# A tile of its own for the normalised tokens of a half, and attention pairs inserted one FFN step sooner

## The chip, the cores and the metric

The kernel runs on one core of one Trainium2 chip. The metric is device microseconds (us) of one execution. TensorE (PE) does the matrix products, VectorE (DVE) and ScalarE (ACT) the elementwise work, GpSimd (POOL) small helpers, and SyncE (SP) issues every transfer (DMA).

## The reference, cut to what matters

```python
# attention: 8 batches, 8 heads, 512 local + 32 global tokens, head dim 64
s_ll = np.where(abs(pos_q - pos_k) <= 32, scale * q_l @ k_l.T, -1e9)
a_l = softmax(concat([scale * q_l @ k_g.T, s_ll]))      # local queries: global keys + a band
out_l = a_l @ concat([v_g, v_l])
out_g = softmax(scale * q_g @ concat([k_g, k_l]).T) @ concat([v_g, v_l])
x = concat([out_g, out_l])                               # (8, 544, 512)
# feed-forward part (FFN), 512 -> 2048 -> 512
xn = (x - mean(x)) / sqrt(var(x) + 1e-6) * g_ln
out = x + relu(xn @ w_ch1) @ w_ch2
```

## The kernel before, in words

A **half** is 256 local tokens of one batch. Two halves make a **chunk** of 512 tokens. There are nine chunks: 0 to 7 of local tokens, and chunk 8 with the 256 global tokens. `ffn(c, ...)` runs the FFN of chunk c over 16 **FFN steps** f (`for f in range(NF)`), one for each block of 128 of the 2048 hidden columns. Values and weights are split into a high and a low part, so each product is three matmuls. Step f has two parts on PE: `mm1(f)`, 12 matmuls of 512 columns (L673), into one of two PSUM banks `ph`, after which ACT writes `hh` (relu, L681) and DVE `hl` (the rest, L682); and `mm2(f - 1, t)` for the four token tiles t, 12 matmuls (L692) that read hh and hl of the step before. Step 0 has no mm2, and after step 15 comes `mm2(15, t)` by itself, with the residual added by DVE (L723) and the rows stored.

The attention for chunk c + 1 is done during the FFN of chunk c. Its unit is a `Pair`, two pairs of heads of one half, four units to a chunk. Code that a unit needs is a generator, and `step()` advances the generator at the head of the queue `side` by one piece: three times in each mm1 and once ahead of each mm2(.., t), so seven times in an FFN step. `attend(u, before, spread)` is such a generator: it issues the scores of pair u (PE L378, 64 small matmuls), the value products of the pair before it (PE L443), their normalisation into `x` (DVE L461), the mask and minimum of the scores (DVE L397) with the exponentials (ACT L407), and then, in chunks 1 to 6, 32 transposes of 32-row blocks on DVE (L430), two to a piece. `at`, filled by `put(place, run)`, says where a generator starts: place 2f + k is step f, ahead of mm1 (k = 0) or ahead of its mm2 (k = 1). In chunks 1 to 6 it is `put(2 * f + 1, ...)` for f in `PAIR_STEPS`; in chunk 0, where the weights are still being split by DVE and ACT, it is a spacing of its own, and the transposes are a second generator (`u.transposes`).

When the pair that ends a half has its values, its `values()` stores the 256 rows to a DRAM scratch `xs` (L335, read back as residual by L701 at step 14 of the chunk's own FFN) and then runs `norm`: statistics (DVE L188, L190), the reciprocal root (POOL L192, L193), a small product (DVE L198), and two ACT activations that write the normalised tokens (L203). `attend` places these with

```python
ends = before.at[1] == HP - 2 if before else False
...
if ends and n in (0, 5, 7):
    next(sums, None)                 # n=0: store, statistics; 5: L198 and L203; 7: second L203
elif next(turns, turns) is turns:    # two block transposes on DVE
    break
```

The tiles `x` come from `new_x()`, a ring of buffers. At step 15 `next_chunk()` transposes the normalised tokens of chunk c + 1 on PE (L621, four times four matmuls, one group ahead of each mm2(14, t)); each group takes one of two PSUM banks `t` (tag `att`, shared with the scores), which ACT (`xh`, L633) and DVE (`xl`, L634) empty.

The order of SP's queue and, from chunk 0 on, of PE is the program's order. For DVE, ACT and POOL it is the program's order in chunks 1 to 6; ahead of these and behind them a scheduler orders their instructions. Chunk 7 has the attention of the global tokens (`Global`) inserted, from its first FFN step on.

Of the kernel before, what the change touches and what calls it, by code (L numbers as in the profile page):

```python
# [17 lines left out]
AF = mybir.ActivationFunctionType  # L18
# [12 lines left out]
SPLIT_AHEAD = 3  # L31
LOADS_AHEAD = 2

PAIR_STEPS = (1, 5, 9, 13)
BIG = 3.0e38


# [8 lines left out]
def attention_ffn_kernel(  # L46
# [130 lines left out]

        return load, split

    def norm(x, js, xn=None):  # L180

        n = len(js)
        at = slice(js[0], js[-1] + 1)
        mv = small.tile([P, 2, 2], F32, name="mv")
        rs = small.tile([P, 2, 2], F32, name="rs")
        st = small.tile([P, 2, 1, 6], F32, name="st")
        for j in js:
            nc.vector.bn_stats(st[:, j, 0, :], x[:, j, :])  # L188
        for j in js:
            nc.vector.bn_aggr(mv[:, j, :], st[:, j])  # L190
        y = rs[:, 0, at]
        nc.gpsimd.tensor_scalar(y, mv[:, at, 1], EPS, None, ALU.add)  # L192
        nc.gpsimd.tensor_tensor(y, y, neg_half[:, :n], op=ALU.pow)  # L193

        def apply():
            yield
            if xn is None:
                nc.vector.scalar_tensor_tensor(  # L198
                    rs[:, 1, at], mv[:, at, 0], -1.0, rs[:, 0, at], ALU.mult, ALU.mult
                )  # L200
            for j in js:
                if xn is None:
                    nc.scalar.activation(  # L203
                        x[:, j, :], x[:, j, :], AF.Identity,
                        bias=rs[:, 1, j:j + 1], scale=rs[:, 0, j:j + 1],
                    )
                else:
                    nc.vector.tensor_scalar(
                        xn[:, j, :], x[:, j, :], mv[:, j, 0:1], rs[:, 0, j:j + 1],
                        ALU.subtract, ALU.mult,  # L210
                    )
                yield

        return apply()

    xtags = cycle(["x0", "x1", "x2"])

    def new_x():
        return fpool.tile([P, 2, DM], F32, name="x", tag=next(xtags))

    class Local:
# [76 lines left out]
        def values(self):  # L298
            b, hp, half = self.at

            pv = self.bank(3, "pv")
            for h in range(2):
                for qb in range(2):
                    for g in range(4):
                        gp = slice(g * WIN, (g + 1) * WIN)
                        nc.tensor.matmul(
                            pv[gp, qb * P + h * D:qb * P + h * D + D],
                            self.pt[:, 2 * h + qb, gp],
                            self.v[:, 4 * qb + g, h * D:(h + 1) * D],
                            start=True,  # L310
                            stop=True,
                            tile_position=(0, g * WIN),
                            skip_group_check=True,
                        )
            ri = small.tile([P, 4], F32, name="ri")
            nc.gpsimd.tensor_scalar(ri, self.sm, SUM_EPS, None, ALU.add)
            nc.vector.reciprocal(ri, ri)
            nc.vector.tensor_tensor(
                self.x[:, :, hp * P:(hp + 1) * P].rearrange("p q (h d) -> p q h d", h=2),
                pv[:, :256].rearrange("p (q h d) -> p q h d", q=2, h=2),  # L320
                ri.rearrange("p (h q) -> p q h", h=2).unsqueeze(3).to_broadcast([P, 2, 2, D]),
                op=ALU.mult,
            )
# [13 lines left out]
    class Pair:  # L337
# [96 lines left out]
        def values(self):  # L434
            b, hp, half = self.at
            pv = ps_h.tile([P, 512], F32, name="pv", tag="ph")
            for j in range(2):
                for h in range(2):
                    for qb in range(2):
                        for g in range(4):  # L440
                            gp = slice(g * WIN, (g + 1) * WIN)
                            at = (2 * j + qb) * P + h * D
                            nc.tensor.matmul(  # L443
                                pv[gp, at:at + D],
                                self.pt[:, j, 2 * h + qb, gp],
                                self.v[:, j, 4 * qb + g, h * D:(h + 1) * D],
                                start=True,
                                stop=True,
                                tile_position=(0, g * WIN),
                                skip_group_check=True,  # L450
                            )
            ri = small.tile([P, 2, 4], F32, name="ri2")
            nc.gpsimd.tensor_scalar(ri, self.sm, SUM_EPS, None, ALU.add)
            if self.next_pair:
                self.next_pair.load_values()
            else:
                begin(1)
            yield
            nc.vector.reciprocal(ri, ri)
            for j in range(2):  # L460
                nc.vector.tensor_tensor(  # L461
                    self.x[:, :, (hp + j) * P:(hp + j + 1) * P].rearrange(
                        "p q (h d) -> p q h d", h=2
                    ),
                    pv[:, j * 256:(j + 1) * 256].rearrange("p (q h d) -> p q h d", q=2, h=2),
                    ri[:, j].rearrange("p (h q) -> p q h", h=2)
                    .unsqueeze(3).to_broadcast([P, 2, 2, D]),
                    op=ALU.mult,
                )
            yield  # L470
            if hp == HP - 2:
                store_x(b, half, self.x)
                yield from norm(self.x, range(2))

    def load_global_keys(ap, bg, hp):
        kr = ap.tile([P, BG, SA], F32, name="gk")
# [285 lines left out]
    ready = {}  # L762
# [41 lines left out]
    def attend(u, before, spread):  # L804

        sums = values(before) if before else iter(())
        scores = u.scores() if u else iter(())
        next(scores, None)
        next(sums, None)
        next(scores, None)  # L810
        next(sums, None)
        yield
        for _ in scores:
            yield
        turns = u.transposes() if u and spread else iter(())
        ends = before.at[1] == HP - 2 if before else False
        n = 0
        while True:
            if ends and n in (0, 5, 7):
                next(sums, None)  # L820
            elif next(turns, turns) is turns:
                break
            n += 1
            yield
        for _ in sums:
            pass
# [60 lines left out]
    for c, chunk in enumerate(chunks):  # L887
        if c == 0:
            ctx.enter_context(tc.manual_schedule(engines={ET.PE}))
        if c == 1:  # L890
            ctx.enter_context(tc.manual_schedule(engines={ET.SP}))
            rest = ExitStack()
            rest.enter_context(tc.manual_schedule(engines={ET.DVE, ET.Activation, ET.Pool}))
        if c == last_chunk - 1:
            rest.close()
        if chunk is None:
            rows = [rows_global(bg) for bg in range(NBG)]
        else:
            rows = [rows_local(b, 2 * half + j) for b, half in chunk for j in range(2)]
        at = {}  # L900

        def put(place, run):
            at.setdefault(min(int(place), 2 * NF - 1), []).append(run)

        if c == 0:
            for n in range(len(PAIR_STEPS) + 1):
                u, before = new.pop(0)
                put(1 + 6.5 * n, lambda u=u, before=before: attend(u, before, False))
                put(3 + 6.5 * n, u.transposes)
        elif c < last_chunk - 1:  # L910
            for f in PAIR_STEPS:
                u, before = new.pop(0)
                put(2 * f + 1, lambda u=u, before=before: attend(u, before, True))
        elif c < last_chunk:
            for n, u in enumerate(phases[1]):
                for o, run in enumerate(global_stages(u)):
                    put(1 + 3.5 * n + o, run)

        def stage(f, k, at=at, c=c):
            if c == 0 and k == 0:  # L920
                for _ in weights_to(f + SPLIT_AHEAD + 1, LOADS_AHEAD):
                    pass
            for run in at.get(2 * f + k, ()):
                yield from run()

        nxt = []

        def next_chunk(c=c, nxt=nxt):
            if c + 1 < len(chunks):
                yield from transpose_chunk(tiles(c + 1), nxt)  # L930

        ffn(c, xt, rows, stage, next_chunk)
        xt = nxt
# [89 lines left out]
```

## Time and profile before

| what | us |
|---|---|
| median of three runs | 987.63 (985.41 to 989.88) |
| the profiled execution | 988.89 |
| its span, first to last instruction | 987.1 |
| PE busy in the span | 933.2 |
| DVE busy | 571.0 |
| ACT busy | 312.9 |

The profiled execution lasts 1.8 us longer than its span, and is 1.3 us above the median. Engines run side by side, each in its own order; an engine that stands still costs time only where the one that sets the end waits for it. The granted clock is TensorE's, as a share of full speed (1.00 is 2.4 GHz, 0.50 is 1.2 GHz), as a mean over a stretch.

### The profile page before, as it was taken

The numbers are of one execution on the slowest core, as the hardware profiler recorded it, in microseconds if no ns is written. First come the engines' busy times: TensorE is split into PE (matmuls) and PEld (weight loads), VectorE is DVE, ScalarE is ACT, GpSimd is POOL, SyncE is SP. The second block draws the span as 40 slices with busy tenths as digits, with TensorE's granted clock in tenths as the row PEclk, the third lists the DMA queues.
The fourth block names the chain that finished last, engine by engine and source line by source line (L and its number), as shares of the span: only waits on it lengthen the run. The fifth ranks groups of instructions, "written<-read, shape, count | busy, mean of one in ns | idle before, by whom it ended". The sixth has DMA issues, their size and how long they took to land.

```text
span 987.1 us, 20917 instructions
## 1 busy us (share of the span) xinstructions
PE 933.2 (95%) x8616; PEld 732.2 (74%) x8616; DVE 571.0 (58%) x1845; ACT 312.9 (32%) x842; POOL 38.4 (4%) x122
## 2 busy tenths in 40 slices
PE   6579998999999998999899999999899989999997
PEld 3348776887878886888688878778787866766796
DVE  4688966647585666666685758474866442222311
ACT  5677843222232322222322232222222121232210
POOL 3100100000000000000000000000000000000000
PEclk9769998999999998999999999999999999999999
DMA  8565542322332222222432243214322324544200
GB/s 355 203 256 195 220 156 93 115 93 71 136 114 91 73 82 97 72 93 72 136 114 93 72 136 115 93 72 136 112 69 80 134 105 147 191 142 140 92 27 21
DMA packets 39039, 118.78 MB, mean 120 GB/s; under 512 B 4256, under 2 KB 6304, under 8 KB 34848
## 3 DMA queue, kind: packets, MB, share of 16 engines
q1 hardware_dynamic: 38944, 117.46, 33.9%
q8 instruction: 67, 1.10, 0.4%
q14 instruction: 28, 0.23, 0.1%
HBM read 99.62 MB, written 17.83 MB: 119 GB/s over the span
## 4 chain that ended last, share of the span: by engine, by line
PE 76%; DVE 9%; DMA 9%; ACT 4%; issue 2%; SPq 0%; POOL 0%; ACTq 0%; DVEq 0%
PE acc L692 33%; PE ph L673 33%; DMA xs<-x 5%; DVE pt L430 3%; DMA raw<-in_wd 3%; PE pv L443 2%; PE sc L378 2%; PE pv L547 1%; DVE hl L682 1%; PE t L621 1%; ACT hh L681 1%; PE sc L499 1%; DVE p L397 1%; DMA u<-in_eu 1%; PE t L535 1%
## 5 line engine op out<-in xcount | busy, mean ns | idle before, releaser
L692 PE MATMUL acc<-w,hh 128*128 128x512 f32 x1088 | 347.2, 401 | 0.0
L673 PE MATMUL ph<-xh,w 128*128 128x512 f32 (+1 forms) x1216 | 309.9, 382 | 3.6 <-ACT xh L633 2.6
L682 DVE SCALAR_TENSOR_TENSOR hl<-ph,hh 128x512 fp32r<-128x512 f32 (+1 forms) x144 | 95.3, 662 | 296.5 <-ACT hh L681 295.6
L673 PEld LDWEIGHTS ph<-xh,w 128*128 128x128 f32 x1216 | 217.7, 189 | 54.1 <-ACT xh L633 4.1
L692 PEld LDWEIGHTS acc<-w,hh 128*128 128x128 f32 x1088 | 209.2, 192 | 46.3
L430 DVE STREAM_TRANSPOSE pt<-p 32x128 f32<-32x128 f32 x768 | 232.1, 302 | 11.3
L692 PE MATMUL acc<-w,hl 128*128 128x512 f32 x544 | 226.6, 417 | 0.3 <-DVE hl L682 0.3
L681 ACT ACTIVATE hh<-ph 128x512 fp32r<-128x512 f32 (+1 forms) x144 | 82.2, 570 | 447.0 <-PE ph L673 447.0
L673 PE MATMUL ph<-xl,w 128*128 128x512 f32 x512 | 141.8, 398 | 0.0
L692 PEld LDWEIGHTS acc<-w,hl 128*128 128x128 f32 x544 | 104.7, 192 | 27.0 <-issue 2.6
L673 PEld LDWEIGHTS ph<-xl,w 128*128 128x128 f32 x512 | 96.6, 190 | 25.2 <-issue 1.8
L407 ACT ACTIVATE p<-p,mn 128x128 f32<-128x128 f32 x224 | 87.2, 391 | 27.5 <-DVE mn L397 27.5
L203 ACT ACTIVATE x<-x,rs 128x512 f32<-128x512 f32 x32 | 25.5, 810 | 90.1 <-DMA xs<-x 76.2
L397 DVE CUSTOM_DVE_ANT_0 p<-sc,mask 128x128 f32<-128x128 f32 x224 | 50.8, 284 | 0.0
L621 PE MATMUL t<-ident,x 128*128 128x128 f32 x136 | 26.6, 318 | 22.6 <-DVE xl L634 11.7
L621 PEld LDWEIGHTS t<-ident,x 128*128 128x128 f32 x136 | 19.3, 161 | 31.8 <-DVE xl L634 14.3
L407 ACT ACTIVATION_READ_ACCUMULATOR p<-p,mn 128x1 f32 x224 | 42.0, 187 | 0.0
L633 ACT ACTIVATE xh<-t,g_sb 128x512 fp32r<-128x512 f32 (+1 forms) x40 | 24.6, 621 | 31.0 <-PE t L621 30.8
L634 DVE SCALAR_TENSOR_TENSOR xl<-t,g_sb,xh 128x512 fp32r<-128x512 f32 (+1 forms) x36 | 24.1, 687 | 16.0 <-ACT xh L633 15.9
L378 PEld LDWEIGHTS sc<-e 64*32 64x32 f32 x1792 | 25.5, 107 | 10.5 <-issue 10.5
L378 PE MATMUL sc<-e 64*32 64x128 f32 x1792 | 33.2, 279 | 0.0
L443 PE MATMUL pv<-v,pt 128*32 128x64 f32 x1792 | 30.8, 220 | 0.0
(72 smaller groups left out, 497.7 us busy)
## 6 DMA issues: line engine op xcount, KB each, us to landing
v<-in_eu SPq DMA_DIRECT2D x28, 1024.0 KB, 7.2
e<-in_eu SPq DMA_DIRECT2D x28, 672.0 KB, 4.5
raw<-in_wd SPq DMA_DIRECT2D x16, 1024.0 KB, 5.4
gk<-in_gk SPq DMA_DIRECT2D x8, 1088.0 KB, 5.0
xs<-x SPq DMA_DIRECT2D x32, 256.0 KB, 7.0
ob<-xs SPq DMA_DIRECT2D x32, 256.0 KB, 6.9
out<-ob SPq DMA_DIRECT2D x32, 256.0 KB, 2.0
gv<-in_gv SPq DMA_DIRECT2D x8, 1024.0 KB, 4.9
```

Of the source, the lines that this page charges most:

```text
L203: nc.scalar.activation(x[:, j, :], x[:, j, :], AF.Identity, bias=rs[:, 1, j:j + 1], scale=rs[:, 0, j:j + 1],)
L378: nc.tensor.matmul(sc[h][gp, at:at + P], self.e[hd, j, w * WIN:(w + 1) * WIN], self.e[hd, j, k0 * WIN:(k0 + 4) * WIN], start=True, stop=Tr ...
L397: nc.vector.tensor_tensor_reduce(out=self.p[:, j, c], in0=sc[h][:, at:at + P], in1=masks[half, qb], scale=-QSCALE, scalar=BIG, op0=ALU.add ...
L407: nc.scalar.activation(self.p[:, j, c], self.p[:, j, c], AF.Exp, bias=mn[:, j, c:c + 1], scale=-1.0, accum_out=self.sm[:, j, c:c + 1],)
L430: nc.vector.transpose(out=self.pt[rp, j, :, gp], in_=self.p[gp, j, :, rp])
L443: nc.tensor.matmul(pv[gp, at:at + D], self.pt[:, j, 2 * h + qb, gp], self.v[:, j, 4 * qb + g, h * D:(h + 1) * D], start=True, stop=True, t ...
L621: nc.tensor.transpose(t[:, j * P:(j + 1) * P], xn[j][:, kt * P:(kt + 1) * P], ident)
L633: nc.scalar.activation(hi, t[:, :n], AF.Copy, scale=gk)
L673: nc.tensor.matmul(ph[:, :n], w[:, kt, :], xx[kt][:, :n], start=(i == 0), stop=(i == 3 * KT - 1),)
L681: nc.scalar.activation(hh[:, :n], ph[:, :n], AF.Relu)
L682: nc.vector.scalar_tensor_tensor(hl[:, :n], ph[:, :n], 0.0, f32(hh[:, :n]), ALU.max, ALU.subtract)
L692: nc.tensor.matmul(acc[t], a[:, ts], w, start=(f == 0 and i == 0), stop=(f == NF - 1 and i == 2),)
```

## The change

A pair that ends a half now writes its normalised tokens to a tile of its own (`xn`, which takes the place of `x` in `ready`), where before the activation wrote over `x`. The ring of tiles has four where it had three; a chunk takes four tiles in place of two. The activation is the same ACT instruction with another output. Second, the attends of chunks 1 to 6 start at FFN steps 0, 4, 8 and 12 in place of 1, 5, 9 and 13, and in chunk 0 at places 1, 7, 13, 19, 25 in place of 1, 7, 14, 20, 27 (their transposes at 3, 9, 15, 21, 27 in place of 3, 9, 16, 22, 29). Local units of chunk 0 and the global tokens keep their norm.

```diff
-PAIR_STEPS = (1, 5, 9, 13)
+PAIR_STEPS = (0, 4, 8, 12)
...
-    def norm(x, js, xn=None):
+    def norm(x, js, xn=None, act=False):
...
-            if xn is None:
+            if xn is None or act:
                 nc.vector.scalar_tensor_tensor(
                     rs[:, 1, at], mv[:, at, 0], -1.0, rs[:, 0, at], ALU.mult, ALU.mult
                 )
             for j in js:
-                if xn is None:
+                if xn is None or act:
                     nc.scalar.activation(
-                        x[:, j, :], x[:, j, :], AF.Identity,
+                        (xn if act else x)[:, j, :], x[:, j, :], AF.Identity,
                         bias=rs[:, 1, j:j + 1], scale=rs[:, 0, j:j + 1],
                     )
...
-    xtags = cycle(["x0", "x1", "x2"])
+    xtags = cycle(["x0", "x1", "x2", "x3"])
...
             if hp == HP - 2:
                 store_x(b, half, self.x)
-                yield from norm(self.x, range(2))
+                xn = ready[self.chunk][-1] = new_x()
+                yield from norm(self.x, range(2), xn, True)
...
-                put(1 + 6.5 * n, lambda u=u, before=before: attend(u, before, False))
-                put(3 + 6.5 * n, u.transposes)
+                put(1 + 6 * n, lambda u=u, before=before: attend(u, before, False))
+                put(3 + 6 * n, u.transposes)
```

## Rows read from the trace of the kernel before

**Rows 1.** The page, part 1: busy time of the engine, share of the span, instructions.
```profile
PE 933.2 (95%) x8616; PEld 732.2 (74%) x8616; DVE 571.0 (58%) x1845; ACT 312.9 (32%) x842; POOL 38.4 (4%) x122
```
**Rows 2.** Windows, chunks 0 to 6, cut where each chunk's mm1(0) starts.
```profile
core 0: us, PE busy (x) PEld busy (x) DVE busy (x) ACT busy (x) POOL busy (x), PEclk, DMA share, GB/s
...
72.70:179.17 106.47, 101.89 (x911) 80.94 (x910) 81.03 (x181) 60.49 (x124) 5.43 (x8) 0.95 0.44 159
179.17:281.42 102.25, 100.87 (x914) 80.64 (x913) 64.54 (x229) 28.23 (x88) 2.83 (x8) 1.00 0.29 98
281.42:388.35 106.93, 103.78 (x913) 82.84 (x913) 69.09 (x241) 28.16 (x88) 2.83 (x8) 0.97 0.28 98
388.35:494.68 106.33, 102.69 (x914) 81.88 (x913) 68.31 (x238) 28.16 (x88) 2.82 (x8) 0.98 0.29 96
494.68:596.92 102.24, 100.86 (x913) 80.70 (x913) 67.64 (x237) 28.24 (x88) 2.82 (x8) 1.00 0.28 98
596.92:702.36 105.44, 102.59 (x913) 81.85 (x913) 69.17 (x241) 28.23 (x88) 2.82 (x8) 0.98 0.29 99
702.36:802.53 100.17, 99.90 (x849) 79.72 (x849) 60.19 (x199) 24.96 (x72) 2.58 (x7) 1.00 0.29 100
```
**Rows 3.** Waits of the whole span: us in total, times, longest.
```profile
ACT x L203 <- DMA xs<-x: 76.2, 13, 7.3
...
PE t L621 <- DVE xl L634: 11.7, 5, 3.1
```
**Rows 4.** Timeline, end of chunk 2: start, us, engine, line, idle before.
```profile
364.39 1.19 SPq L335 DMA_DIRECT2D xs<-x  x2
...
369.05 0.16 DVE L198 SCALAR_TENSOR_TENSOR rs<-mv,rs 128x2 f32<-128x2 f32 x1
...
373.09 0.82 ACT L203 ACTIVATE x<-x,rs 128x512 f32<-128x512 f32 x1 [6.83 <-DMA xs<-x]
...
374.42 0.69 DVE L682 SCALAR_TENSOR_TENSOR hl<-ph,hh 128x512 fp32r<-128x512 f32 x1 [5.21 <-ACT hh L681]
...
375.14 3.79 DVE L430 STREAM_TRANSPOSE pt<-p 32x128 f32<-32x128 f32 x12
...
378.96 0.69 DVE L682 SCALAR_TENSOR_TENSOR hl<-ph,hh 128x512 fp32r<-128x512 f32 x1
379.57 1.40 DVE L634 SCALAR_TENSOR_TENSOR xl<-t,g_sb,xh 128x512 fp32r<-128x512 f32 x2
...
380.37 1.12 PE L621 MATMUL t<-ident,x 128*128 128x128 f32 x4 [3.06 <-DVE xl L634]
```
**Rows 5.** Windows, right behind that stall of chunk 2.
```profile
381.00:385.00 4.00, 4.00 (x14) 3.31 (x13) 1.38 (x2) 1.37 (x2) 0.00 (x0) 0.50 0.01 4
```
**Rows 6.** Timeline, last pair and end of chunk 1.
```profile
257.86 1.09 PE L673 MATMUL ph<-xh,w 128*128 128x512 f32 x4
...
259.61 0.69 DVE L682 SCALAR_TENSOR_TENSOR hl<-ph,hh 128x512 fp32r<-128x512 f32 x1 [4.91 <-ACT hh L681]
259.96 1.10 PE L443 MATMUL pv<-v,pt 128*32 128x64 f32 x64
...
266.80 0.16 DVE L198 SCALAR_TENSOR_TENSOR rs<-mv,rs 128x2 f32<-128x2 f32 x1
...
268.83 0.82 ACT L203 ACTIVATE x<-x,rs 128x512 f32<-128x512 f32 x1 [4.83 <-DMA xs<-x]
...
271.37 1.10 PE L673 MATMUL ph<-xh,w 128*128 128x512 f32 x4
...
276.11 0.66 PE L621 MATMUL t<-ident,x 128*128 128x128 f32 x4 [1.38 <-DVE xl L634]
```
**Rows 7.** Timeline, end of chunk 0, DVE and PE.
```profile
166.45 0.69 DVE L682 SCALAR_TENSOR_TENSOR hl<-ph,hh 128x512 fp32r<-128x512 f32 x1
...
167.83 0.16 DVE L198 SCALAR_TENSOR_TENSOR rs<-mv,rs 128x2 f32<-128x2 f32 x1
...
165.06 0.38 PE L621 MATMUL t<-ident,x 128*128 128x128 f32 x2
168.90 0.47 PE L621 MATMUL t<-ident,x 128*128 128x128 f32 x1 [3.45 <-ACT x L203]
...
179.01 1.10 PE L673 MATMUL ph<-xh,w 128*128 128x512 f32 x4
```
**Rows 8.** Timeline, end of chunk 6, from its first transposes to chunk 7's mm1(0).
```profile
794.93 0.60 PE L621 MATMUL t<-ident,x 128*128 128x128 f32 x4
...
802.37 1.10 PE L673 MATMUL ph<-xh,w 128*128 128x512 f32 x4
```
**Rows 9.** Windows, start of chunk 7, with a global unit inserted at step 0.
```profile
803.00:809.00 6.00, 4.00 (x42) 2.02 (x41) 2.44 (x9) 0.82 (x2) 0.00 (x0) 1.00 0.36 126
809.00:815.00 6.00, 5.33 (x22) 4.35 (x22) 0.75 (x5) 2.51 (x6) 0.23 (x1) 0.72 0.50 186
```

## The prediction

> **What bounds the kernel.** I read the page first: PE is busy 95% of the span [rows 1], so time can be won only where PE stands still or runs at half clock. Next the windows by chunk [rows 2]. Chunks 1 to 5 do the same work, yet last 102.2 to 106.9 us, and the long ones are those with a granted clock below 1.00. Chunk 6 lasts 100.2 and loses almost nothing. So several microseconds hang on something that happens in some chunks and not in others. The waits name it [rows 3]: PE's large wait is that of the transposes L621 for `xl` (11.7 us in five waits), one at the end of each of chunks 1 to 5, and on ACT the activation L203 waits 76.2 us for the store of `xs`.
>
> The timeline of chunk 2's end links the two [rows 4]. The store of x is issued at 364.39. The scale for L203 is ready at 369.05 + 0.16 = 369.21, but L203 writes over x and so starts only at 373.09, when the store has read it. ACT takes its instructions in order, so the `hh` of step 14 behind it is late, `hl` starts at 374.42, and twelve block transposes queued on DVE behind it end at 378.93. Only then come the `hl` of step 15 (378.96) and the first `xl` (379.57). The third group of PE transposes needs the bank that this `xl` empties: PE stands for 3.06 us, until 380.37. Thereafter the clock is 0.50 for a stretch [rows 5]: the stall is paid a second time. In chunk 1 the store was quicker, L203 came 2.0 us behind its scale instead of 3.9, and PE stood only 1.38 us, with the clock at 1.00 over the chunk [rows 2, 6].
>
> **Chunks 1 to 5, what can be won.** Chunk 1 without its stall lasts 102.25 - 1.38 = 100.87. Against that, chunks 1 to 5 lose 1.4, 6.1, 5.5, 1.4 and 4.6 us [rows 2], 18.9 in all. The price of a stall: 3.06 us of standing cost 6.1 in chunk 2.
>
> **Own tile.** It adds no instruction: the same activation writes elsewhere, at 0.82 us as before [rows 4]. It takes away L203's wait for the store; what ends its wait next is L198. The new tile could bring a wait of its own if the ring came round too soon. With four tiles to a chunk and four in the ring, each tile is written once a chunk: the raw x of a half is last read by its own store and activation, some 100 us before it is written again; the normalised tile is read by the transposes at step 15 and written again some five FFN steps later at the earliest. I cost that at nothing. The waits of L203 in mid-chunk (the half that ends there) cost PE nothing today, as no other large wait of PE is listed, so their removal is worth nothing.
>
> **One step sooner, end of chunk.** An attend takes 21 calls of `step()` (one, then n = 0 to 19), and an FFN step makes seven. From step 13 on, 4 + 7 + 3 = 14 calls come ahead of hh(15), and the other seven are spent in mm2(15) and the next chunk. From step 12 on, all 21 come ahead of hh(15): the last twelve block transposes (12 x 0.31 = 3.8 us) leave the stretch where DVE must empty the transposes' banks, but lie ahead of hl(15). Does DVE get through in time? Counted on chunk 1's rows [rows 6], as if all lay one step later than it will: L198 ends at 266.96; L203 follows and ends at 267.8, hh(13) at 268.3, hl(13) at 269.0; twelve transposes to 272.9; mm1(14) ends at 272.5, so hh(14) at 273.1, hl(14) at 273.8; twelve transposes to 277.7. mm1(15) ends 5.6 us behind mm1(14), at 278.1, and hl(15) can start at 278.7. DVE is free 1.0 us before it is wanted. Then the end of the chunk goes as in chunk 6, which has no pair to transpose there: 7.44 us from the first transposes to the next mm1(0) [rows 8]. I leave 0.3 us a chunk for what is not quite hidden: 18.9 - 1.5 = 17.4.
>
> **One step sooner, start of chunk.** The first attend now starts behind mm1(0), where no mm2 follows. PE goes mm1(0), scores and values (about 2.1 us: 259.96 + 1.10 less 258.95 [rows 6]), mm1(1). mm1(1) takes the bank that mm1(0) filled, as the value products hold the other, so it needs hl(0). On the rows of an attend in mid-chunk, hl ends at 259.61 + 0.69 = 260.30 and the value products at 261.06: 0.76 us to spare, covered by the small matmuls alone, where now mm2's 2.8 us cover it as well. If hl(0) were late, each us would be a us of PE in each of six chunks. DVE ahead of it has the four residual sums of the chunk before, each ready as its mm2(15, t) ends; the last is ready 2.8 us ahead of mm1(0)'s end, so I take nothing here, with rival A as the upper bound. hl(1) is next: it lies behind eight L397, the two L461 and twelve transposes, ends about 8.4 us behind mm1(0), and is read by mm2(1), about 10.5 us behind it (2.1, then mm1(1), mm2(0), mm1(2) at 2.8 each): 2 us to spare.
>
> The skill speaks against this insertion. The page Perfetto Trace Analysis, section Tensor Engine Instruction (MATMUL, LD_WEIGHTS), says that VectorE and ScalarE keep strict order, so that whatever an attend puts on DVE ahead of hl(1) delays it, with nothing slipping past. Chunk 2's end agrees: hh of step 14 waited behind L203. By the rule alone, without the 2 us to spare, that is rival A.
>
> The moved steps also move their DMAs: for each attend the loads of the next pair's e and v, and for the two that end a half the two stores. At step 12 they leave SP's queue 5.6 us ahead of the residual loads of step 14 instead of right among them, and those are wanted only at the chunk's end. At step 0 they stand behind the output stores, which wait for the residual sums and are through before the scores end; e and v are wanted four FFN steps (over 22 us) later. Nothing either way.
>
> **Chunk 0.** PE spends 179.01 - 165.06 = 13.95 us from the first transposes to the next mm1(0) [rows 7], chunk 6 only 7.44 [rows 8]: 6.5 us lost, at a clock of 0.95 over the chunk [rows 2]. Here L203 waits not for the store but for L198 at 167.83, which DVE does among the block transposes. With the last attend two places sooner all this comes 5.6 us earlier: L198 at 162.2, L203 done by 164, ahead of 165.06. But DVE's order in chunk 0 is the scheduler's, and hl, which today waits at 166.45 in a place that costs little, may move to one where PE wants it. Bounds: 0 and 6.5; I take 4.5, nearer the upper one, as the whole group only shifts.
>
> **Chunks 7 and 8** keep their order: 0, with 1 us either way for the scheduler's choices.
>
> **Sum.** 17.4 + 4.5 = 21.9 us off the profiled execution: 988.9 - 21.9 = 967.0. The median lies 1.3 lower, which makes 965.7; I forecast 966.
>
> **Rivals.**
> A, the insertion at step 0 becomes a stall, and the kernel slower. For it: the one insertion at step 0 that a steady chunk shows, that of a global unit in chunk 7, leaves PE busy 4.00 of 6.00 us, and the clock falls to 0.72 in the next stretch [rows 9]: 2.0 us idle and about 1.7 us lost to the clock (0.28 x 6), 3.7 in all. Against it: a global unit needs its score banks twice and its transposes on PE, a pair neither. The gain is used up at 21.9 / 6 = 3.7 us a chunk, so by that price the time is 989, no change. At the price of chunk 2's stall, 6.1 a chunk, it is 967.0 + 36.6 = 1004. The skill's page TensorE: Matmul & The Clock Gate, section What's actually happening, has the clock at half after idling, which agrees with the 0.50 of rows 5.
> B, the DVE remains late at the end of the chunk, by more than the 1.0 us counted, and chunk 0 is not mended. Then 1.4 us stay in each of five chunks, as chunk 1 has now, and 6.5 in chunk 0: 988.9 - 18.9 + 7.0 = 977.
> C, the change does not do what it says: L203 still waits for something as late as the store (a ring tile, L198), and PE's stalls stay: 988. Against it: the scale is there 3.9 us before the start in chunk 2 [rows 4].
>
> **Numbers.** Forecast 0.73 (962 to 971 by itself), B 0.15, A 0.08 (half of it slower, half no change), C 0.04. About 0.5% is what a measurement of this kernel can tell from no change. Faster by more 0.88, within it 0.08, slower 0.04. The range: the low end takes all 25.4 us (18.9 + 6.5) off 987.6 and 2 us of spread between runs, 960; the high end is B, 977.
>
> **What would show it.** Right: chunks 1 to 5 all last about 101 us at a clock of 1.00; PE's waits of L621 for xl fall from 11.7 to under 2 us; L203's waits for the store are gone but for those of the prologue and the global tokens; L621 of chunk 0 no longer waits for L203. Wrong: PE idle behind mm1(0) waiting for hl(0) or for a score bank, a clock of 0.5 at the start of chunks, or xl still last at their end. The weakest points are the 0.76 us at step 0 and the scheduler's order in chunk 0.

## The result and the profile after

The changed kernel takes 964.3 us (median of four runs, 962.7 to 965.8), the kernel before, now also measured four times, 988.75 us (985.4 to 993.4). The ratio is 0.975 (95% interval 0.970 to 0.980). The profiled execution has a span of 960.9 us where it was 987.1: 26.2 us less.

The windows of the changed kernel, cut as those of before [rows 2] where each chunk's mm1(0) starts, here from chunk 0 to chunk 7 (us, busy time of PE, PEld, DVE, ACT and POOL, granted clock, DMA share, GB/s):

```profile
53.50:172.39 118.89, 110.11 (x1007) 86.81 (x1007) 98.29 (x215) 76.18 (x153) 4.53 (x9) 0.95 0.50 178
172.39:273.07 100.68, 100.68 (x913) 80.67 (x912) 68.35 (x239) 28.23 (x88) 2.83 (x8) 1.00 0.30 102
273.07:373.76 100.69, 100.69 (x913) 80.66 (x912) 68.36 (x239) 28.22 (x88) 2.82 (x8) 1.00 0.31 102
373.76:474.44 100.68, 100.68 (x914) 80.67 (x912) 68.38 (x239) 28.23 (x88) 2.82 (x8) 1.00 0.30 102
474.44:575.13 100.69, 100.69 (x914) 80.67 (x913) 68.37 (x239) 28.22 (x88) 2.83 (x8) 1.00 0.30 102
575.13:675.80 100.67, 100.67 (x913) 80.67 (x912) 68.36 (x239) 28.23 (x88) 2.82 (x8) 1.00 0.31 102
675.80:775.41 99.61, 99.61 (x850) 79.79 (x849) 57.20 (x191) 25.04 (x72) 2.59 (x7) 1.00 0.29 101
775.41:909.33 133.92, 129.10 (x1353) 92.59 (x1352) 38.28 (x127) 33.26 (x70) 3.35 (x12) 0.99 0.41 141
```

Chunks 1 to 5, which differed by up to 4.7 us, now agree to 0.02 us; PE is busy all of their time, at a clock of 1.00. Their sum is 503.4 us in place of 523.2 [rows 2]: 19.8 us, three quarters of the whole gain. Chunk 6 gives 0.6. Chunk 0 is 118.89 us here, from its first mm1 at 53.50. The first line of [rows 2] starts at 72.70, but chunk 0 of before starts at 53.17: it lasts 125.84 us, at a clock of 0.91 and not the 0.95 of that line. So these two profiles differ by 7.0 us in it. The stretch from chunk 7 to the end of the span is 0.8 us longer, and what lies ahead of chunk 0's mm1(0) 0.3 us. -19.8 - 0.6 - 7.0 + 0.8 + 0.3 makes -26.3, the span's change but for rounding.

The waits of the whole span, changed kernel (us in total, times, longest):

```profile
ACT x L203 <- DVE rs L198: 46.8, 14, 7.7
...
ACT x L203 <- DMA xs<-x: 12.0, 2, 7.3
```

The activation L203 waited 76.2 us in 13 places for a store [rows 3], 11 of them in chunks 1 to 6. Those 11 are gone: there it now waits for L198, its scale. The two that are left are both in chunk 7, at the global tokens, which keep their norm. PE's 11.7 us for `xl` are gone from its list altogether.

The first of the two that are left shows the same chain still at work, with the score matmuls (L500) at its end:

```profile
834.32 0.16 DVE L198 SCALAR_TENSOR_TENSOR rs<-mv,rs 128x1 f32<-128x1 f32 x1 [1.00 <-POOL rs L193]
...
838.33 0.82 ACT L203 ACTIVATE x<-x,rs 128x512 f32<-128x512 f32 x1 [7.34 <-DMA xs<-x]
...
839.66 0.69 DVE L683 SCALAR_TENSOR_TENSOR hl<-ph,hh 128x512 fp32r<-128x512 f32 x1 [5.18 <-ACT hh L682]
...
840.76 1.05 PE L500 MATMUL sc<-gk,gq 64*32 64x272 f32 x16 [1.43 <-DVE gp L510]
```

L203 starts 3.85 us behind its scale, hh and hl behind it are late, DVE empties a score bank (L510) late, and PE waits 1.43 us for that bank. How long this wait is varies with the store: in the run with chunk 0's old spacing below, L203 waited 9.68 us here and PE 3.77.

The end of chunk 2 in the timeline of the changed kernel, to lay beside [rows 4]:

```profile
350.62 1.04 SPq L335 DMA_DIRECT2D xs<-x  x2
...
355.28 0.16 DVE L198 SCALAR_TENSOR_TENSOR rs<-mv,rs 128x2 f32<-128x2 f32 x1
355.47 0.82 ACT L203 ACTIVATE x<-x,rs 128x512 f32<-128x512 f32 x1 [2.99 <-DVE rs L198]
...
356.80 0.69 DVE L683 SCALAR_TENSOR_TENSOR hl<-ph,hh 128x512 fp32r<-128x512 f32 x1 [1.36 <-ACT hh L682]
...
362.38 3.79 DVE L430 STREAM_TRANSPOSE pt<-p 32x128 f32<-32x128 f32 x12
...
367.22 0.69 DVE L683 SCALAR_TENSOR_TENSOR hl<-ph,hh 128x512 fp32r<-128x512 f32 x1 [1.05 <-ACT hh L682]
```

L203 starts 0.03 us behind the end of its scale, where it was 3.9. The store, issued at 350.62 and landed 7.2 us later, is still under way then, and nobody waits for it. At hl(15) (367.22) DVE has stood idle for 1.05 us: the prediction had counted that it would be free 1.0 us before it is wanted.

The start of chunk 3, with the pair inserted at step 0:

```profile
375.62 1.10 PE L674 MATMUL ph<-xh,w 128*128 128x512 f32 x4
...
377.38 0.69 DVE L683 SCALAR_TENSOR_TENSOR hl<-ph,hh 128x512 fp32r<-128x512 f32 x1 [2.73 <-ACT hh L682]
377.74 1.10 PE L443 MATMUL pv<-v,pt 128*32 128x64 f32 x64
...
378.77 1.20 PE L674 MATMUL ph<-xh,w 128*128 128x512 f32 x4
```

hl(0) ends at 378.07, 0.70 us before mm1(1) wants its bank. The cover is thin, but it holds: PE's list of waits has none for an hl in chunks 1 to 6. hl(1) ends 8.4 us behind mm1(0) and is read 10.6 us behind it, as was counted (8.4 and 10.5).

The end of chunk 0, DVE and PE, to lay beside [rows 7]:

```profile
158.50 0.69 DVE L683 SCALAR_TENSOR_TENSOR hl<-ph,hh 128x512 fp32r<-128x512 f32 x1
159.22 0.63 DVE L430 STREAM_TRANSPOSE pt<-p 32x128 f32<-32x128 f32 x2
159.88 0.16 DVE L198 SCALAR_TENSOR_TENSOR rs<-mv,rs 128x2 f32<-128x2 f32 x1
...
159.24 0.50 PE L693 MATMUL acc<-w,hl 128*128 128x512 f32 x1 [1.99 <-DVE hl L683]
...
164.95 0.60 PE L622 MATMUL t<-ident,x 128*128 128x128 f32 x4
...
172.39 1.10 PE L674 MATMUL ph<-xh,w 128*128 128x512 f32 x4
```

DVE's group of block transposes, statistics and one hl stands in the same order as before, 7.95 us earlier. So the transposes on PE no longer wait, and 164.95 to 172.39 is 7.44 us where it was 13.95. But the hl that lay late in that group is now the one of step 13, and PE waits 1.99 us for it, a wait that it did not have before. In this execution the clock stays at 1.00 behind that wait; the last section shows executions in which it does not.

### The profile page after: what moved, and what is told of

Its sections match the earlier page's. It is cut to its first block, busy times and chain, and to the rows that moved or that the text cites. A ratio compares the mean times of both kernels' runs of the same rounds, so it can differ in the third digit from the quotient of the medians.

```text
span 960.9 us, 20910 instructions
## 1 busy us (share of the span) xinstructions
PE 921.9 (96%) x8616; PEld 725.3 (75%) x8616; DVE 570.7 (59%) x1845; ACT 312.8 (33%) x842; POOL 36.9 (4%) x122
## 4 chain that ended last, share of the span: by engine, by line
PE 89%; DVE 3%; DMA 3%; ACT 2%; issue 1%; SPq 1%; POOL 0%; ACTq 0%; DVEq 0%
PE acc L693 39%; PE ph L674 39%; PE sc L378 3%; PE pv L443 3%; DMA raw<-in_wd 2%; PE t L622 1%; PE pv L548 1%; PE sc L500 1%; DVE pt L430 1%; DMA u<-in_eu 1%; PE t L536 1%; PE tp L422 0%; ACT raw L138 0%; PE sc L258 0%; DVE hl L683 0%
## 5 line engine op out<-in xcount | busy, mean ns | idle before, releaser
L693 PE MATMUL acc<-w,hh 128*128 128x512 f32 x1088 | 342.6, 396 | 0.0
L693 PEld LDWEIGHTS acc<-w,hh 128*128 128x128 f32 x1088 | 205.6, 189 | 45.4
L693 PE MATMUL acc<-w,hl 128*128 128x512 f32 x544 | 223.0, 410 | 2.0 <-DVE hl L683 2.0
L693 PEld LDWEIGHTS acc<-w,hl 128*128 128x128 f32 x544 | 102.5, 188 | 27.8 <-issue 2.6
L203 ACT ACTIVATE x<-x,rs 128x512 f32<-128x512 f32 x32 | 25.6, 812 | 58.8 <-DVE rs L198 46.8
L635 DVE SCALAR_TENSOR_TENSOR xl<-t,g_sb,xh 128x512 fp32r<-128x512 f32 (+1 forms) x36 | 24.5, 689 | 11.1 <-ACT xh L634 11.1
L443 PEld LDWEIGHTS pv<-v,pt 128*32 128x32 f32 x1792 | 26.3, 110 | 5.7 <-issue 5.3
L622 PE MATMUL t<-ident,x 128*128 128x128 f32 x136 | 23.1, 293 | 6.2 <-DVE x L208 5.6
```

What stands on the lines that cost most here:

```text
L203: nc.scalar.activation((xn if act else x)[:, j, :], x[:, j, :], AF.Identity, bias=rs[:, 1, j:j + 1], scale=rs[:, 0, j:j + 1],)
L443: nc.tensor.matmul(pv[gp, at:at + D], self.pt[:, j, 2 * h + qb, gp], self.v[:, j, 4 * qb + g, h * D:(h + 1) * D], start=True, stop=True, t ...
L622: nc.tensor.transpose(t[:, j * P:(j + 1) * P], xn[j][:, kt * P:(kt + 1) * P], ident)
L693: nc.tensor.matmul(acc[t], a[:, ts], w, start=(f == 0 and i == 0), stop=(f == NF - 1 and i == 2),)
```

## The experiments

Two questions were open. Which of the two edits does what, since each by itself could free the end of a chunk? And is it really the store that L203 waited for? In all the experiments "T" is the theory that the store's wait holds back hh, hl and with them xl, and that chunk 0's gain is that of its spacing. A chunk's length is always from its mm1(0) to the next chunk's. Ratios are to the kernel before, run beside on the same chip.

**Own tile alone.** The changed kernel with

```diff
-PAIR_STEPS = (0, 4, 8, 12)
+PAIR_STEPS = (1, 5, 9, 13)
...
-                put(1 + 6 * n, lambda u=u, before=before: attend(u, before, False))
-                put(3 + 6 * n, u.transposes)
+                put(1 + 6.5 * n, lambda u=u, before=before: attend(u, before, False))
+                put(3 + 6.5 * n, u.transposes)
```

> Own tile, places as before (1, 5, 9, 13; 6.5 in chunk 0). Theory T (the two edits overlap: either takes most of the stall at the end of chunks 1 to 5, and chunk 0's gain comes from its spacing alone): L203 follows L198, the hl of step 14 is early, the twelve block transposes ahead of hl(15) end as hl(15) is wanted, so chunks 1 to 5 last 100.7 to 101.3 us each and chunk 0 keeps its 6.5 us loss: about 969 to 971 us. Rival S (the earlier steps do it all, the tile nothing): chunks 1 to 5 stay at 102 to 107 us, 988 us. Rival W (the tile does it all, chunk 0 too): 963 to 965 us.

Measured: 966.1 us, 0.977 (0.974 to 0.979). Its windows of chunks 1 and 2, and DVE at the end of chunk 2:

```profile
177.65:278.38 100.73, 100.73 (x913) 80.70 (x912) 64.63 (x229) 28.25 (x88) 2.84 (x8) 1.00 0.29 100
278.38:379.12 100.74, 100.74 (x913) 80.68 (x912) 68.48 (x239) 28.25 (x88) 2.83 (x8) 1.00 0.30 102
```
```profile
366.18 0.16 DVE L198 SCALAR_TENSOR_TENSOR rs<-mv,rs 128x2 f32<-128x2 f32 x1
367.70 0.69 DVE L683 SCALAR_TENSOR_TENSOR hl<-ph,hh 128x512 fp32r<-128x512 f32 x1 [1.36 <-ACT hh L682]
368.43 3.79 DVE L430 STREAM_TRANSPOSE pt<-p 32x128 f32<-32x128 f32 x12
372.58 0.69 DVE L683 SCALAR_TENSOR_TENSOR hl<-ph,hh 128x512 fp32r<-128x512 f32 x1 [0.36 <-ACT hh L682]
373.19 0.74 DVE L635 SCALAR_TENSOR_TENSOR xl<-t,g_sb,xh 128x512 fp32r<-128x512 f32 x1
```

All of chunks 1 to 5 last 100.73 or 100.74 us. The twelve block transposes still lie ahead of hl(15), as at 375.14 before [rows 4], but start in time and are done 0.36 us before hl(15) is wanted. Rival S falls. The transposes of chunk 0 on PE still wait 3.45 us for L203 (13.06 us from the first of them to the next mm1(0), 5.6 more than with the whole change), so rival W falls in its mechanism. T's total, 969 to 971 us, was missed: T priced chunk 0's loss at the full 6.5 us, and the part on chunk 0 below shows that the new spacing wins less. Chunk 0 is 123.4 us, 2.5 less than before, of which only 0.9 lie at its end, and chunk 7 is 132.3. In the repetition further down, chunk 0 of one and the same kernel differs by 2.3 us between two profiles, so I read nothing into these differences.

**Steps alone.** The changed kernel with

```diff
-    xtags = cycle(["x0", "x1", "x2", "x3"])
+    xtags = cycle(["x0", "x1", "x2"])
...
-                xn = ready[self.chunk][-1] = new_x()
-                yield from norm(self.x, range(2), xn, True)
+                yield from norm(self.x, range(2))
```

> Earlier places, normalised in place with three tiles. Theory T: L203 still waits for the store, two steps further from the end; what DVE has queued behind the late hl catches up in part. Chunks 1 and 4 (store quick) about 101 us, chunks 2, 3 and 5 (store slow, hl(15) about 2 us late) 102.5 to 104.5; chunk 0 gains its 6 to 7 us. 970 to 976 us. Rival S (steps do it all): every chunk 100.7, 964 us. Rival W (the tile does it all): chunks 1 to 5 as before, 982 to 988 us.

Measured: 973.8 us, 0.985 (0.981 to 0.988). Windows of chunks 1 to 5, and the end of chunk 2:

```profile
173.53:275.70 102.17, 100.91 (x914) 80.69 (x913) 68.29 (x239) 28.24 (x88) 2.84 (x8) 1.00 0.30 100
275.70:379.56 103.86, 101.40 (x913) 80.53 (x912) 68.27 (x239) 28.02 (x88) 2.83 (x8) 1.00 0.30 99
379.56:481.72 102.16, 101.15 (x914) 80.59 (x913) 68.31 (x239) 28.19 (x88) 2.83 (x8) 1.00 0.30 100
481.72:584.56 102.84, 101.16 (x914) 80.64 (x913) 68.28 (x239) 28.24 (x88) 2.83 (x8) 1.00 0.30 100
584.56:688.81 104.25, 101.14 (x914) 80.59 (x912) 68.28 (x239) 28.13 (x88) 2.84 (x8) 1.00 0.29 98
```
```profile
358.65 0.16 DVE L198 SCALAR_TENSOR_TENSOR rs<-mv,rs 128x2 f32<-128x2 f32 x1
362.60 0.81 ACT L203 ACTIVATE x<-x,rs 128x512 f32<-128x512 f32 x1 [6.74 <-DMA xs<-x]
...
363.94 0.69 DVE L682 SCALAR_TENSOR_TENSOR hl<-ph,hh 128x512 fp32r<-128x512 f32 x1 [5.12 <-ACT hh L681]
364.68 0.50 PE L692 MATMUL acc<-w,hl 128*128 128x512 f32 x1 [0.37 <-DVE hl L682]
368.47 0.69 DVE L682 SCALAR_TENSOR_TENSOR hl<-ph,hh 128x512 fp32r<-128x512 f32 x1
373.01 0.69 DVE L682 SCALAR_TENSOR_TENSOR hl<-ph,hh 128x512 fp32r<-128x512 f32 x1
374.42 0.66 PE L621 MATMUL t<-ident,x 128*128 128x128 f32 x4 [1.59 <-DVE xl L634]
```

The wait for the store is there as before. What is late is now the hl of step 13, one FFN step further from the end than the hl(14) of before (one, not the two that were expected). Behind it, at 363.94, come hl(14) and hl(15) at distances of 4.5 us, twelve transposes and one hl each, with no idle time between, while PE's steps are 5.6 us or more: the delay shrinks by about one us a step and is not yet gone at hl(15). PE now waits in two places, 0.37 us for hl(13) and 1.59 for xl. The stalls stay short and the clock at 1.00. Each chunk keeps 1.5 to 3.6 us of loss, so by themselves the earlier steps win 7.9 of the 19.8 us of chunks 1 to 5. That is T in its sum. Chunks 1 and 4 lose a us or two more than it said and chunk 3 a little less; L203 was held behind its scale for other times here than in the profile of before (2.8 us in chunk 1, where it had been 1.9). Chunk 0's end takes 7.42 us, as with the whole change.

**The store, without the tile.** The kernel before, where the two stores read a constant tile:

```diff
+    other = const.tile([P, 2, DM], F32, name="other")
+    nc.gpsimd.memset(other, 0.0)
...
-                store_x(b, half, self.x)
+                store_x(b, half, other)
                 yield from norm(self.x, range(2))
```

> The kernel before (three tiles, normalised in place, old places), but the two stores of a pair's half read a constant tile instead of x, so that L203 has no store to wait for. It leaves out the true residual and output rows of chunks 1 to 7: its output is not the reference's. Theory T (of the tile, only the absence of the wait for the store counts): chunks 1 to 5 last 100.7 us each as with the own tile alone, chunk 0's end keeps its loss, 965 to 968 us. Rival (the new tile helps by something else, such as an activation that does not write where it reads, or the fourth buffer): chunks 1 to 5 stay at 102 to 107 us, 983 to 990 us.

Measured: 965.1 us, 0.978 (0.975 to 0.981), with chunks 1 and 2 as follows:

```profile
175.41:276.14 100.73, 100.73 (x913) 80.67 (x912) 64.63 (x229) 28.25 (x88) 2.84 (x8) 1.00 0.30 100
276.14:376.87 100.73, 100.73 (x913) 80.66 (x912) 68.44 (x239) 28.26 (x88) 2.83 (x8) 1.00 0.31 102
```

This kernel leaves out the true residual rows and serves for its time alone. It has three buffers, an activation that writes over its input, and the same number and size of transfers, and its chunks last what they last with the own tile. This is the run that shows the cause: writing in place costs nothing here, writing over what a transfer is still reading does.

**Chunk 0's old spacing.** The changed kernel with 6.5 for 6 in the two lines of `put`.

> The changed kernel with chunk 0's old spacing (6.5). Theory T: chunks 1 to 6 stay at 100.7 us, and chunk 0 loses its 6.5 us at the end again, L198 late behind block transposes: 970 to 972 us. Rival W (chunk 0's gain comes from the tile, as L203 there no longer waits for a store): 963 to 965 us.

Measured: 967.1 us, 0.978 (0.975 to 0.981). Chunks 1 to 5 last 100.67 or 100.68 us; chunk 0's end has its 13.83 us again, with the same 3.45 us wait for L203. So the tile does not mend chunk 0, and the new spacing does. The total that T gave, 970 to 972 us, was missed. Against the run with nothing at step 0 (below, 963.5 us on the same chip, with the new spacing) the spacing is worth 3.6 us by the medians, not 6.5, but the two intervals overlap, and the profile of this run also has a chunk 7 of 137.4 us, where the other's is 133.8 (the wait for the store at the global tokens, above).

The windows of all profiles say more. Chunk 0 lasts 122.6 to 125.8 us in the four with the old spacing (before, own tile alone, the store without the tile, this run) and 118.9 to 121.5 us in the eight with the new one. The two groups do not meet, and their means lie 3.7 us apart. Of the 6.5 us that the end gains, 2 us and more go into the wait for hl(13).

**Closer still in chunk 0.** A spacing of 5.5 for 6 in the same lines.

> The changed kernel with a spacing of 5.5 places in chunk 0 (attends at 1, 6, 12, 17, 23; transposes at 3, 8, 14, 19, 25). Theory (chunk 0's end is already free of its loss; the 2.0 us that mm2(13) waits for hl(13) is the price of the scheduler's order, which moves along): no gain at the end, a wait of 2 us for another hl, total 962 to 967 us. Rival (sooner is better): the wait for hl goes and chunk 0 is 2 to 3 us shorter, 961 to 962 us.

Measured: 964.3 us, 0.978 (0.975 to 0.980). The end of the chunk takes 7.37 us, and PE waits 2.04 us for an hl, one FFN step sooner; chunk 0 as a whole is 122.2 us. The price moves along, as the theory says: it belongs to the order on DVE, not to the place.

**Nothing at step 0.** `PAIR_STEPS = (1, 4, 8, 12)`.

> The changed kernel with places (1, 4, 8, 12), so nothing is inserted at step 0 of chunks 1 to 6. Theory T (insertion at step 0 is covered by the 0.76 us to spare, at no cost): same time within 0.3%, chunks 100.7 us, no wait of mm1(1). Rival A (insertion at step 0 costs something that the gain hides, up to 0.5 us a chunk): 3 us faster, 961 us. The other way, if the step-0 place is needed: three steps between the first two attends leave DVE late, some chunks longer, 966 us or more.

Measured: 963.5 us, 0.974 (0.971 to 0.977); chunks 1 to 5 last 100.67 to 100.69 us. The insertion at step 0 neither costs nor gives anything that can be measured.

**Old places in chunks 1 to 6,** new spacing in chunk 0, own tile; and beside it on the same chip the changed kernel again.

> The changed kernel with the old places in chunks 1 to 6 (1, 5, 9, 13); chunk 0 keeps its new spacing, the tile stays. Theory T (with the tile, the places in chunks 1 to 6 are worth 0.05 us a chunk, and what the earlier steps add to the tile is chunk 0's): chunks 1 to 5 last 100.7 us, chunk 0 ends without its loss, within 0.2% of the changed kernel beside it. Rival (the earlier places in chunks 1 to 6 bring what own tile alone lacks): 966 to 968 us, 0.2 to 0.4% slower than it.

> The changed kernel itself, again, for comparison on the same chip with the next one: 0.975 of the kernel before.

Measured: 964.4 us (0.979; 0.976 to 0.981) with the old places, 963.3 us (0.978; 0.975 to 0.981) for the changed kernel. The intervals overlap. By the chunks the difference is plain: 100.72 to 100.74 us against 100.68 to 100.69, some 0.05 us each. With the tile there, the earlier places in chunks 1 to 6 are worth no more than that. Two profiles of the changed kernel also show what a chunk 0 can vary by: 118.89 us in the first, 121.18 here.

**The global units of chunk 7, one and two places later.** This follows rival A's row [rows 9]: the one insertion at step 0 that does cost something.

```diff
-                    put(1 + 3.5 * n + o, run)
+                    put(2 + 3.5 * n + o, run)
```

> The changed kernel with the global units of chunk 7 inserted one place later (2 + 3.5 n + o): the first no longer falls into step 0, where no mm2 follows. Theory: an insertion at step 0 costs only where it needs a bank twice or has PE transposes behind it, as the global unit does; moved, PE's 2.7 us idle at the start of chunk 7 and the half clock behind it go, chunk 7 lasts 129 to 131 us in place of 133.9, about 961 us. Rival (the last global unit, one place later as well, is late for the transposes of chunk 8): what is won at the start is lost at the end, 964 us or more.

> The same, two places later (3 + 3.5 n + o), so that the first global unit starts ahead of mm2(0) at step 1. Theory: as one place later, 129 to 131 us for chunk 7, 960 to 962 us. Rival as there, more so: the last unit's normalisation comes at step 14 and its stores delay it, chunk 8's transposes wait 2 to 4 us, 964 to 967 us.

> The changed kernel with the global units one place later, again. Theory: chunk 7 lasts 129 to 130 us in place of 134, ratio to the kernel before 0.970 to 0.973, below that of the changed kernel by 0.004 to 0.005. Rival (the earlier difference was spread between runs): no difference.

Measured: one place later 960.0 us (0.973; 0.970 to 0.975), and again 959.9 us (0.974; 0.971 to 0.978) beside the changed kernel's 963.3; two places later 961.9 us (0.975). Chunk 7 lasts 129.3 us in both runs with one place and 129.9 with two, against 133.9 and 133.4. In the ten profiles with the old place, chunk 7 lasts 131.9 to 137.4 us. The start of chunk 7, first the changed kernel, then one place later (the second of its two runs):

```profile
775.00:781.00 6.00, 4.85 (x47) 2.87 (x45) 2.70 (x7) 0.60 (x1) 0.00 (x0) 1.00 0.52 186
781.00:787.00 6.00, 4.41 (x22) 3.47 (x16) 1.52 (x7) 2.74 (x6) 0.23 (x1) 0.72 0.52 186
```
```profile
777.00:783.00 6.00, 5.97 (x45) 3.76 (x50) 2.94 (x8) 0.60 (x1) 0.00 (x0) 1.00 0.52 186
783.00:789.00 6.00, 6.00 (x43) 4.52 (x28) 2.21 (x8) 3.11 (x7) 0.23 (x1) 1.00 0.53 186
```

PE's idle 2.7 us and the lower clock are gone, and nothing is lost at the end: from chunk 7's end to the last instruction it is 51.6 us in all of them. About 1 us of the gain lies elsewhere, in the middle of the chunk. L203 waits only 2.3 us for its store there, where it waited 7.2, and PE's wait for the score bank falls from 1.30 to 0.31 us. One place later is the fastest version here, 3.4 us below the changed kernel beside it, where the chunk's windows give 4.1 us. The intervals of the two ratios overlap, and the difference, 0.003, is below the 0.004 to 0.005 that were expected. But each of its five runs (959.4 to 962.0 us) lies below each of the five of the changed kernel (962.2 to 966.2).

## Why the prediction was right

**What bounds it.** Right. PE's stall at the end of chunks 1 to 5 was the time to be won, its price in the long chunks was the stall and the half clock behind it, and the store was its origin, which the run with another source for the store shows by itself. (The 2.0 us read for L203 in chunk 1 is 1.9, counted as the 3.9 of chunk 2 is; nothing hangs on it.)

**Chunks 1 to 5.** The term was 17.4 us, with 18.9 as the most; they gave 19.8. The 0.3 us a chunk that were held back were not needed: where the chain is early enough, PE waits for nothing. And a clean chunk is 100.68 us, not the 100.87 taken from chunk 1.

**Which edit.** Here the prediction was loose. It took away the wait by the tile and the last twelve transposes by the steps, and summed one gain for both. The runs show that the tile alone gives 19.5 of the 19.8 us, as DVE is then in time for hl(15) with transposes ahead of it (0.36 us), and that the steps alone leave 1.5 to 3.6 us a chunk. In chunks 1 to 6 the steps add 0.05 us a chunk to the tile.

**Start of chunk.** Costed at nothing with 0.76 us to spare; 0.70 was there, and the run without it has the same chunks. Rival A did not come. Its row of chunk 7 was a true price, but of a unit that needs its banks twice and its transposes on PE, and moving that unit gave some 3 of the 4.1 us by which chunk 7 got shorter.

**Chunk 0.** The end was forecast to lose its 6.5 us, with an hl that may move to where PE wants it: both came, 6.5 and 1.99 us. The term was 4.5; the means of the profiles with either spacing lie 3.7 us apart, and the 7.0 us by which the first two profiles differ take the longest chunk 0 of one group and the shortest of the other. The mechanism was right, but 4.5 was a choice between two bounds and not worked out, so that it came near is in part luck. Over the whole kernel 21.9 us was forecast and 24.5 measured by the medians: the large term was 2.4 us too small and this one 0.8 too large, and the two misses go against each other.

**Chunks 7 and 8.** Costed at nothing, 1 us either way; 0.8 us was lost. What varies there, the wait for the store at the global tokens, the prediction did not name.

**Rivals B and C** did not come: DVE was free 1.05 us before hl(15), and L203 follows its scale at once.

The Trainium skill's rule that VectorE and ScalarE keep strict order (Perfetto Trace Analysis, section Tensor Engine Instruction (MATMUL, LD_WEIGHTS)) was cited against the insertion at step 0. The trace agrees with it, but what it cost was decided elsewhere, at chunk 2's end [rows 4]: an activation that waits for a store, 3.9 us beyond its scale, holds back an hh whose own operands are there.

## What to carry to other kernels

An instruction that overwrites a tile waits for the transfers that still read it (L203 in chunks 1 to 6 of before: 1.7 to 4.3 us beyond its scale), and what stands behind it on its engine waits as well. Give the result a tile of its own when a store of the input has just been issued. Read the price of a stall where it ends (here the wait passes from ACT to DVE and ends at PE's transposes). Compare equal stretches of work: five equal chunks with unequal lengths showed how much could be won before any cause was known. When two edits aim at one stall, run each alone: here the tile did nearly all of it in chunks 1 to 5, and the earlier steps next to nothing beside it. And look for the same wait where the change does not reach: at the global tokens it is still there.

## What the hardware showed that was not expected

Single waits of PE of up to 1.6 us left the clock at 1.00 (chunks 1 to 5 of the steps alone, all at 1.00), and one of 3.06 us was followed by a stretch at 0.50 [rows 5]. In between, one and the same wait went either way. The wait of 1.97 to 1.99 us for hl(13) at the end of chunk 0 is in all eight profiles with the new spacing. Over the 4 us behind it the clock was 1.00 in five of them and 0.57 in the other three. Here the changed kernel, first profile and repetition:

```profile
159.24:163.24 4.00, 4.00 (x17) 3.27 (x18) 1.44 (x4) 2.00 (x3) 0.00 (x0) 1.00 0.00 0
```
```profile
161.37:165.37 4.00, 4.00 (x11) 3.14 (x12) 1.44 (x4) 2.00 (x3) 0.00 (x0) 0.57 0.00 0
```

The FFN step with the wait lasts 7.9 us in the first case and 9.4 in the second. That is 1.5 of the 2.3 us by which chunk 0 differs between these two profiles; what made the clock fall in one and not in the other, the runs do not show.

At the start of chunk 7, two waits close together, 1.15 us for a score bank and 1.51 us for the exponentials, came with a mean clock of 0.72 over 6 us, and with both gone it was 1.00. So two short waits near each other can be followed by the lower clock as one long one is; no run has one of the two without the other.

With no wait left, a chunk of some 900 PE instructions repeats to 0.02 us within a profile.
